# A kernel that counts its PE instructions and keeps loads of data out of a stretch of each 256

## The chip, the cores and the metric

One Trainium2 chip, one core. The metric is the device time of one execution in microseconds (us). The kernel before took 297.31 us, the median of three timed runs (295.42, 297.31 and 297.91).

The engines are named as the profile names them: PE (matmuls; PEld are its weight loads, from the same queue), DVE, ACT, POOL, and SP, which issues all DMA transfers here.

## The reference

Eight sequences of 3584 tokens, 192 channels, in two stages, all in float32. First each token's window of 7 tokens is summed with weights that are a softmax over the 7 taps, for 8 heads of 24 channels. Then a soft mixture of 8 experts with 4 slots each works on all 28672 tokens at once:

```python
# stage 1
w = softmax(weight_gen, axis=-1)                       # (B, S, 8 heads, 7 taps)
out = np.einsum('bshk,bskhg->bshg', w, x_unf)          # windows of 7 tokens
# stage 2, x is the output of stage 1 as (28672, 192)
logits = x @ phi                                       # 192 x 32
d = softmax(logits, axis=0)                            # over all tokens
slot_input = d.T @ x
slot_out[e] = np.maximum(slot_input[e] @ w1[e], 0) @ w2[e]
c = softmax(logits, axis=1)                            # over the 32 slots
return c @ slot_out
```

## The kernel before

The tokens are cut into 280 groups of 104 (35 for each sequence). One long loop runs over 70 slots of four groups (`SLOTS`). For each slot PE does the windowed sum as matmuls with banded weights (`conv`, line 264), ACT takes the result out of PSUM (`conv_out`), PE transposes it (`xpose`, line 284), ACT takes it out again. For every four slots, a unit, PE makes the logits (`logits`, line 340), DVE, PE, POOL and ACT find their running maximum and the exponentials, DVE turns these into `dt` (`dturn`, line 399), and PE sums the slot inputs (`dispatch`, line 418). In parallel the taps of later groups go through `chain`: DVE takes the maximum (`tap_top`, line 189), POOL subtracts, ACT takes the exponential, POOL and DVE sum and divide, POOL spreads them into `wide`, and DVE transposes them into the bands (`tap_turn`, line 237). After the loop come the experts (`hidden`, `outputs`) and the output stage: matmuls, eviction and stores.

Transfers of the loop, all issued by SP in one queue. `loadx` (line 162) brings the tokens: 56 slots of data in four quarters each, into four places in turn, so quarter h of slot t+4 can start when PE is through with slot t. `loadw` (line 165) brings the raw taps, 35 of them into four buffers. `loadw1` (line 485) and `loadw2` (line 488) bring the experts' weights, the latter into the places of tokens that are done with.

The order around the change is made by a planner. `op` records each piece of work with its engine and a cost in us, `model` and `times` lay them out in time, and the result `at[i]` is the planned start of piece i. The kernel is then written out in the order of `at` (lines 823 to 838). Each engine runs its own queue in that order. For PE's pieces `steps` notes the planned time at which each PE instruction ends. A load planned for later than `PACED`, 24 us, is tied by `paced` (line 818) to the PE instruction that the plan has just finished at that time: SP waits for that instruction's semaphore before it issues the load. The last eight loads of `loadw2` are left for after the loop (`later`).

A matmul in float32 shows as two weight loads and two matmuls in the trace (2,240 calls of line 264 as 4,480 of each), a transpose as one of each.

Of the kernel before, what the change touches and what calls it, by code (L numbers as in the profile page):

```python
# [33 lines left out]
PACED = 24.0  # L34
# [3 lines left out]
WGAP = 0.68  # L38
TR = 3 * 32 + T
RESTAT = 4  # L40
BEHIND = 8
ROUNDS = {"TE": 8, "SP": 12}
VSUM = ()
# [13 lines left out]
def conv_soft_moe(ctx, tc, xh, wh, phi, w1a, w1b, w2, out):  # L57
# [188 lines left out]
    def unit(p):  # L246
        return next((u, p - p0) for u, (p0, n) in enumerate(UNITS) if p < p0 + n)
# [250 lines left out]
    ops, writer, readers = [], {}, {}  # L498

    def op(eng, cost, reads, writes, f, *a, late=0.0, due=None):  # L500


        i = len(ops)
        preds = {writer[r] for r in (*reads, *writes) if r in writer}
        for r in writes:
            preds |= set(readers.get(r, ()))
            writer[r], readers[r] = i, []
        for r in reads:
            readers.setdefault(r, []).append(i)
        preds.discard(i)  # L510
        ops.append((eng, cost, late + 0.1 * (eng == "TE"), preds, due, f, a))
# [27 lines left out]
    VE, AC, PO, TE, SP = "VE", "AC", "PO", "TE", "SP"  # L539
# [141 lines left out]
    for k in range(SLOTS):  # L681
        u, i = unit(2 * k)[0], unit(2 * k)[1] // 2
# [17 lines left out]
    k = SLOTS - 2  # L700
# [104 lines left out]
    def times(start, bound):  # L805
        at, t = [0.0] * len(ops), 0.0
        for i, o in enumerate(ops):
            at[i] = t
            t += o[1] * (o[0] == bound)
        best = None  # L810
        for _ in range(ROUNDS[bound]):
            at = model(at, start, bound)
            end = max(at[i] for i, o in enumerate(ops) if o[0] == bound)
            if best is None or end < best[0]:
                best = end, at
        return best[1]

    def paced(j, by):
        if j.engine == mybir.EngineType.SP:
            tc.add_manual_dep(j, by.name, mybir.DependencyInfo(  # L820
                mybir.DependencyClass.Sync, mybir.DependencyReason.DATA), reason="paced")

    at = times({TE: 0.0, VE: 3.2, AC: 4.8, PO: 5.0, SP: 0.7}, TE)
    block = nc.cur_bb.bb
    steps, later = [], [(E - 1 - i // 4, 3 - i % 4) for i in range(BEHIND)][::-1]
    for i in sorted(range(len(ops)), key=lambda i: (at[i], i)):
        if ops[i][5] is loadw2 and ops[i][6] in later:
            continue
        n = len(block.instructions)
        ops[i][5](*ops[i][6])  # L830
        new = block.instructions[n:]
        if ops[i][0] == TE:
            new = [j for j in new if j.engine == mybir.EngineType.PE]
            steps += [(at[i] + ops[i][1] * (k + 1) / len(new), j) for k, j in enumerate(new)]
        elif ops[i][0] == SP and at[i] > PACED:
            to = max((t, k) for k, (t, _) in enumerate(steps) if t <= at[i])[1]
            for j in new:
                paced(j, steps[to][1])

    actx.close()  # L840

# [136 lines left out]
    spots += [big[:, NXS * XB - OW :]]  # L978
    assert RESTAT + 2 < len(spots)
    spots += [big[:, i * OW : (i + 1) * OW] for i in range(E * WE // OW)]  # L980
# [46 lines left out]
    def turn_two():  # L1027
        twos[0] += 1
        return ("two", twos[0] % 4)

    for j, (kind, b, g, n) in enumerate(parts):
        two, to = [turn_two(), turn_two()], ("spot", j % len(spots))
        op(TE, (1.1 + 0.8 * kind) * (n + 6) / 24, [("cT", 2 * (b + half) + (g >= STEPS[1][0])) for half in range(1 + kind)]
           + ["sob"] * kind, two, rows, kind, b, g, n, j)
        cuts = ((0, 2, AC), (2, 4, VE)) if j < 3 else ((0, 2, AC), (3, 4, VE), (2, 3, AC))
        free = ["w2"] * (j >= RESTAT + 2)
        for lo, hi, e in cuts:
# [6 lines left out]
        for lo, hi in ((0, 2), (2, 4)) if j < 3 else ((0, 4),):  # L1044
            op(SP, 0.576 * (hi - lo) * n / 18, [], [(to, c[0]) for c in cuts if lo <= c[0] < hi],
               store, j, n, lo, hi, late=2.0)
        if j == RESTAT:
            rest = turn_two()
            op(TE, 1.05, [], [rest], others, 0)
        elif j == RESTAT + 1:  # L1050
            op(TE, 1.05, [], [rest, "w2"], others, 1)
# [3 lines left out]
    at = times({TE: 0.0, VE: 0.65, AC: 0.0, PO: 0.0, SP: 0.0}, SP)  # L1055
# [93 lines left out]
```

## Time and profile before

| | us |
|---|---|
| median of three timed runs | 297.31 |
| the profiled execution's own time | 298.47 |
| its span, first to last instruction | 296.5 |
| PE matmuls busy | 259.1 |
| PE weight loads busy | 212.8 |
| DVE busy | 213.3 |
| ACT busy | 180.3 |
| POOL busy | 160.2 |

The profiled execution is 0.4% above the median of the timed ones; its span leaves out 2.0 us around the first and the last instruction. The loop over slots ends near 214 us by the chain of work that ended last; then come the experts and, from about 235 us, the output stage. The matmuls' ends are modelled, so a busy PE is not PE at its peak. "issue" as the end of a wait means that the profile shows nothing the engine waited for. The queue of DMA packets named "instruction" with the number 8 brings 16 KB packets, 55 in all.

### The profile page before, as it was taken

What the parts mean: (1) busy time and instruction counts of PE and PEld (TensorE: products, weight loads), DVE (VectorE), ACT (ScalarE), POOL (GpSimd) and SP (SyncE); (2) the same over time, 40 slices, a digit from 0 to 9 for tenths busy, and PEclk for the clock granted to TensorE, in tenths of its full rate; (3) what the DMA queues carried; (4) which work ended last, traced back from release to release, by engine and by line L of the source; (5) the groups of instructions that cost most, each with busy time, mean ns of one, the idle gap of its engine ahead of it and who ended that gap; (6) DMA issues with size and microseconds to landing.
All of it is one profiled execution on the core that took longest, in us unless ns stands there. A gap on an engine that the chain in (4) does not pass through costs nothing.

```text
span 296.5 us, 16191 instructions
## 1 busy us (share of the span) xinstructions
PE 259.1 (87%) x7032; PEld 212.8 (72%) x7032; DVE 213.3 (72%) x385; ACT 180.3 (61%) x307; POOL 160.2 (54%) x253
## 2 busy tenths in 40 slices
PE   8899899999999999998999899989989897956510
PEld 8789699888988988897998788979859652312100
DVE  8878799989978977768767778673268598977310
ACT  8887458757766764675666565655322378967430
POOL 9976669659659685475374636620016415455100
PEclk9999999999999999999999999999999999966775
DMA  6877676776767786667767757666898199999994
GB/s 188 215 217 206 204 202 205 206 217 194 213 193 203 213 226 166 189 190 206 204 178 214 218 161 201 187 180 169 259 295 266 45 345 416 412 420 416 415 418 185
DMA packets 31558, 70.11 MB, mean 236 GB/s; under 512 B 5888, under 2 KB 21248, under 8 KB 31488
## 3 DMA queue, kind: packets, MB, share of 16 engines
q1 hardware_dynamic: 31488, 69.08, 73.5%
q8 instruction: 55, 0.90, 1.4%
q14 instruction: 15, 0.12, 0.1%
HBM read 46.70 MB, written 22.36 MB: 233 GB/s over the span
## 4 chain that ended last, share of the span: by engine, by line
PE 76%; issue 5%; DMA 4%; POOL 4%; DVE 3%; ACT 3%; POOLq 0%; ACTq 0%; DVEq 0%
PE ring L264 32%; PE ring L284 16%; PE ls L340 8%; PE acb L418 8%; PE two L991 7%; DMA out<-big 3%; PE ring L901 2%; ACT big L997 2%; PE ring L923 1%; POOL big L434 1%; DMA taps<-wh 1%; POOL LT L106 1%; DVE band L237 1%; DVE cT L476 1%; PE ring L418 0%
## 5 line engine op out<-in xcount | busy, mean ns | idle before, releaser
L264 PE MATMUL ring<-big,band 128*26 128x96 f32 x4480 | 111.3, 248 | 6.4 <-issue 4.9
L264 PEld LDWEIGHTS ring<-big,band 128*26 128x26 f32 x4480 | 100.6, 130 | 14.9 <-issue 9.5
L272 ACT COPY tm<-ring 128x768 f32<-128x768 f32 x68 | 54.4, 800 | 63.4 <-PE ring L264 47.3
L237 DVE STREAM_TRANSPOSE band<-wide 128x832 f32<-128x832 f32 x70 | 70.6, 1026 | 4.4 <-POOL wide L228 3.2
L284 PE MATMUL ring<-ident,tm 122*128 122x122 f32 x408 | 50.8, 273 | 0.4 <-issue 0.4
L228 POOL TENSOR_TENSOR wide<-taps,sum 128x364 f32<-128x364 f32 x32 | 31.4, 981 | 27.5 <-DVE sum L219 10.8
L290 ACT COPY cm<-ring 128x624 f32<-128x624 f32 x68 | 44.1, 690 | 1.7 <-PE ring L284 1.6
L284 PEld LDWEIGHTS ring<-ident,tm 122*128 122x128 f32 x408 | 42.3, 141 | 3.6 <-issue 0.8
L197 POOL TENSOR_TENSOR taps<-taps,top 128x364 f32<-128x364 f32 x34 | 33.2, 980 | 6.9 <-DVE top L189 6.6
L213 POOL TENSOR_TENSOR si<-taps 128x208 f32<-128x208 f32 x34 | 21.8, 641 | 20.5 <-ACT taps L205 20.1
L991 PE MATMUL two<-cT,so 32*128 32x442 f32 (+2 forms) x136 | 21.9, 652 | 12.2 <-DVE cT L476 6.9
L189 DVE TENSOR_REDUCE top<-taps 128x52 f32<-128x364 f32 x34 | 28.0, 825 | 4.2 <-DMA taps<-wh 4.2
L418 PE MATMUL acb<-tm,dt 128*32 128x193 f32 x544 | 26.9, 328 | 1.5 <-DVE dt L399 0.9
L340 PE MATMUL ls<-cm,phi_sb 128*32 128x208 f32 x544 | 27.4, 338 | 0.0
L106 POOL TENSOR_TENSOR LT<-LT,sm 128x576 f32<-128x576 f32 (+1 forms) x16 | 18.1, 1134 | 16.0 <-DVE sm L104 16.0
L94 POOL TENSOR_TENSOR LT<-LT,rm 128x576 f32<-128x576 f32 (+1 forms) x16 | 18.1, 1131 | 15.6 <-DVE rm L92 15.4
L991 PEld LDWEIGHTS two<-cT,so 32*128 32x128 f32 x136 | 8.4, 205 | 22.9 <-ACT big L997 6.2
L219 DVE RECIPROCAL sum<-sum 128x52 f32<-128x52 f32 (+1 forms) x36 | 16.2, 453 | 10.3 <-POOL sum L215 10.1
L205 ACT ACTIVATE taps<-taps 128x364 f32<-128x364 f32 (+1 forms) x36 | 17.9, 501 | 8.2 <-POOL taps L197 8.2
L418 PEld LDWEIGHTS acb<-tm,dt 128*32 128x32 f32 x544 | 17.7, 110 | 5.4 <-issue 1.3
L340 PEld LDWEIGHTS ls<-cm,phi_sb 128*32 128x32 f32 x544 | 16.9, 109 | 5.0 <-issue 0.3
L997 ACT COPY big<-two 128x884 f32<-128x884 f32 (+3 forms) x26 | 17.1, 739 | 3.9 <-issue 3.0
(135 smaller groups left out, 294.3 us busy)
## 6 DMA issues: line engine op xcount, KB each, us to landing
big<-xh SPq DMA_DIRECT2D x224, 120.0 KB, 3.5
taps<-wh SPq DMA_DIRECT2D x35, 182.0 KB, 3.8
out<-big SPq DMA_DIRECT2D x7, 884.0 KB, 10.2
big<-w SPq DMA_DIRECT2D x32, 192.0 KB, 4.1
out<-big SPq DMA_DIRECT2D x6, 936.0 KB, 10.5
w1a_sb<-w1a SPq DMA_DIRECT2D x32, 128.0 KB, 3.5
out<-w1a_sb SPq DMA_DIRECT2D x3, 936.0 KB, 12.1
w1b_sb<-w1b SPq DMA_DIRECT2D x16, 128.0 KB, 3.5
```

Of the source, the lines that this page charges most:

```text
L189: V.tensor_reduce(out=row(m), in_=run(c, 0, KT).rearrange("p k s -> p s k"), axis=AX.X, op=ALU.max)
L197: eng.tensor_tensor(out=t, in0=t, in1=rows7(tops.pop((c, 0))), op=ALU.subtract)
L228: eng.tensor_tensor(out=dst, in0=raw[c % NTAP][:, 0:KT], in1=m.unsqueeze(1).to_broadcast([128, KT, n, T]), op=ALU.mult)
L237: V.transpose(bands[c % NBAND][:, b].rearrange("p b j l -> p (b j l)"), wide[:, b].rearrange("p b j -> p (b j)"))
L264: P.matmul(cv[32 * blk : 32 * blk + T, p % 2, o : o + 4 * GW], bands[g // 8 % NBAND][:, g // 4 % CH, :, i], xbd[:, place(t), :, b * GW : ( ...
L272: copy(tms[tm_at(u)][:, pr + of.start : pr + of.stop, 1 : 2 * D + 1], cv[:, of, 0 : 2 * D])
L284: P.transpose(pt[:, j // 3, o : o + TR], tm[0:TR, pr + j // 3, 1 + o : 129 + o], ident[0:TR, 0:TR])
L290: copy(cm.rearrange("p (a i) (b j) -> p a (i b) j", i=3, j=T), pts["t", k][:, of, 0 : 3 * 128].rearrange("p a (i j) -> p a i j", j=32)[... ...
L340: P.matmul(lp[32 * blk : 32 * blk + 32, lo:hi, par, 0:T], phi_sb[:, 2 * par + i, :], cm[:, lo:hi, 1 if i else 2 * par, blk, :], start=(i = ...
L418: P.matmul(ac[32 * q : 32 * q + 32], dt[:, g, :], tm[:, g // 2, o : o + D + 1], start=(g < 4), stop=(g + 4 >= 2 * n))
L991: P.matmul(pos[j][q // 2][m * half : m * half + m, q % 2, 0 : n * T], of[32 * q : 32 * q + 32], cT[32 * q : 32 * q + 32, g0 : g0 + n, 0:T] ...
L997: copy(to.rearrange("p (q c) -> p q c", c=n * T), pos[j][lo // 2][:, lo % 2 : lo % 2 + hi - lo, 0 : n * T])
```

## The change

While the kernel is written out, each PE instruction gets a running count: four for a matmul, two for a transpose, and 0.045 for semaphore waits, from 7 at the beginning. Loads that the plan starts after 24 us are put into a list `waiting` and written out by `send` when PE's steps have come that far. A load whose step falls on the places 140 to 212 of each 256 by that count (and whose planned time is under 198 us) is tied to the first later step outside of these places. Two loads are at least 0.44 us apart in planned time. A load that another piece needs is written out at once, before that piece. The plan itself (`op`, `model`, `times`) is as before, and so is what each engine computes.

```diff
+ISSUE, OPEN, WAITS, BLOCK, CLOSED = 0.44, 198.0, 0.045, 256, (140, 212)
...
     block = nc.cur_bb.bb
     steps, later = [], [(E - 1 - i // 4, 3 - i % 4) for i in range(BEHIND)][::-1]
+    count = [7.0]
+
+    def counted():
+        for j in block.instructions[seen[0]:]:
+            if j.engine == mybir.EngineType.PE:
+                count[0] += (2 if getattr(j, "is_transpose", False) else 4) + WAITS
+        seen[0] = len(block.instructions)
+
+    seen = [0]
+    counted()
+    waiting, sent = [], [0.0]
+
+    def send(force=False):
+        while waiting:
+            i = waiting[0]
+            t = max(at[i], sent[0] + ISSUE)
+            k = max((t0, k) for k, (t0, _, _) in enumerate(steps) if t0 <= t)[1]
+            if at[i] < OPEN and CLOSED[0] <= (steps[k][2] - 1) % BLOCK < CLOSED[1]:
+                while k < len(steps) and CLOSED[0] <= (steps[k][2] - 1) % BLOCK < CLOSED[1]:
+                    k += 1
+            if not force and (k >= len(steps) - 1 or steps[-1][0] < t):
+                return
+            k = min(k, len(steps) - 1)
+            sent[0] = max(t, steps[k][0])
+            waiting.pop(0)
+            n = len(block.instructions)
+            ops[i][5](*ops[i][6])
+            for j in block.instructions[n:]:
+                paced(j, steps[k][1])
+
     for i in sorted(range(len(ops)), key=lambda i: (at[i], i)):
         if ops[i][5] is loadw2 and ops[i][6] in later:
             continue
+        if ops[i][0] == SP and at[i] > PACED:
+            waiting.append(i)
+            send()
+            continue
+        while any(j in waiting for j in ops[i][3]):
+            send(True)
         n = len(block.instructions)
+        c = count[0]
         ops[i][5](*ops[i][6])
-        new = block.instructions[n:]
         if ops[i][0] == TE:
-            new = [j for j in new if j.engine == mybir.EngineType.PE]
-            steps += [(at[i] + ops[i][1] * (k + 1) / len(new), j) for k, j in enumerate(new)]
-        elif ops[i][0] == SP and at[i] > PACED:
-            to = max((t, k) for k, (t, _) in enumerate(steps) if t <= at[i])[1]
-            for j in new:
-                paced(j, steps[to][1])
+            new = [j for j in block.instructions[n:] if j.engine == mybir.EngineType.PE]
+            counted()
+            steps += [(at[i] + ops[i][1] * (k + 1) / len(new), j, c + (count[0] - c) * (k + 1) / len(new))
+                      for k, j in enumerate(new)]
+            send()
+    send(True)
```

## Rows read from the trace of the kernel before

**Rows 1.** The page: busy us of each engine (share of the span, instructions), and the chain of work that ended last, shares of the span by engine.

```profile
PE 259.1 (87%) x7032; PEld 212.8 (72%) x7032; DVE 213.3 (72%) x385; ACT 180.3 (61%) x307; POOL 160.2 (54%) x253
...
PE 76%; issue 5%; DMA 4%; POOL 4%; DVE 3%; ACT 3%; POOLq 0%; ACTq 0%; DVEq 0%
```

**Rows 2.** The timeline of PE's weight loads in two stretches, 59 to 62 us (the row of 61.19) and 20 to 216 us (the others): start, us, engine, line, operation, tiles, form, count, and in brackets the idle time of the weight loads ahead of it and what ended it.

```profile
32.35 0.26 PEld L264 LDWEIGHTS ring<-big,band 128*26 128x26 f32 x9 [1.59 <-issue]
...
61.19 0.19 PEld L366 LDWEIGHTS acb<-mq,sel 128*32 128x32 f32 x8 [0.66 <-POOL sum L215]
...
86.62 0.60 PEld L264 LDWEIGHTS ring<-big,band 128*26 128x26 f32 x27 [0.37 <-issue]
...
90.39 1.14 PEld L284 LDWEIGHTS ring<-ident,tm 122*128 122x128 f32 x11 [0.19 <-issue]
...
106.94 0.37 PEld L264 LDWEIGHTS ring<-big,band 128*26 128x26 f32 x16 [0.35 <-issue]
...
111.91 0.12 PEld L418 LDWEIGHTS acb<-tm,dt 128*32 128x32 f32 x3 [0.58 <-issue]
...
120.17 1.03 PEld L284 LDWEIGHTS ring<-ident,tm 122*128 122x128 f32 x10 [0.63 <-issue]
...
158.81 0.64 PEld L418 LDWEIGHTS acb<-tm,dt 128*32 128x32 f32 x20 [0.76 <-issue]
...
168.19 0.19 PEld L264 LDWEIGHTS ring<-big,band 128*26 128x26 f32 x5 [1.46 <-issue]
...
185.27 0.69 PEld L264 LDWEIGHTS ring<-big,band 128*26 128x26 f32 x32 [0.79 <-issue]
...
198.34 0.19 PEld L264 LDWEIGHTS ring<-big,band 128*26 128x26 f32 x4 [1.16 <-issue]
```

**Rows 3.** Three stretches: from and to (us), length, then for each engine (PE, PEld, DVE, ACT, POOL) its busy us and the number of its instructions, PE's granted clock, the DMA engines' busy share, GB/s.

```profile
0.00:32.34 32.34, 28.51 (x723) 26.14 (x723) 25.98 (x51) 24.43 (x39) 26.96 (x57) 1.00 0.76 207
...
32.34:168.18 135.84, 132.00 (x4047) 117.58 (x4048) 109.69 (x188) 86.79 (x148) 90.07 (x142) 1.00 0.72 202
...
168.18:197.90 29.72, 28.59 (x886) 25.86 (x885) 22.65 (x38) 17.89 (x30) 14.70 (x25) 1.00 0.63 179
```

**Rows 4.** The instructions of line 264 between 24 and 200 us: the semaphore waits in PE's queue (count; min/median/max ns; first and last start).

```profile
L264 PEldq EVENT_SEMAPHORE  x97: 51/51/51, 27.4 to 198.5; - x97
```

**Rows 5.** Eight stretches of PE, each of about 256 matmuls and weight loads, in the columns of rows 3.

```profile
82.17:86.25 4.08, 4.08 (x130) 3.88 (x125) 3.43 (x8) 2.55 (x5) 3.63 (x7) 1.00 0.70 195
154.06:158.05 3.99, 3.99 (x132) 3.78 (x126) 3.46 (x8) 2.89 (x7) 2.41 (x5) 1.00 0.78 223
...
27.39:30.77 3.38, 3.38 (x131) 3.36 (x125) 3.13 (x6) 2.07 (x4) 3.14 (x7) 1.00 0.82 243
163.32:166.74 3.42, 3.42 (x134) 3.21 (x128) 2.75 (x5) 1.72 (x4) 2.90 (x5) 1.00 0.93 245
181.17:184.48 3.31, 3.31 (x129) 3.06 (x128) 3.05 (x8) 2.08 (x4) 0.85 (x3) 1.00 0.81 218
193.85:197.18 3.33, 3.33 (x136) 3.32 (x129) 2.64 (x6) 1.43 (x3) 1.00 (x1) 1.00 0.71 205
45.33:48.66 3.33, 3.33 (x128) 2.98 (x131) 2.90 (x5) 2.83 (x6) 3.16 (x4) 1.00 0.66 192
40.83:45.31 4.48, 4.48 (x138) 3.93 (x127) 4.45 (x7) 2.79 (x6) 3.44 (x5) 1.00 0.70 195
```

**Rows 6.** The instruction queue's packets that began in four narrow stretches, in this order: 29.90 to 29.93, 41.43 to 41.46, 45.54 to 45.57 and 113.23 to 113.25 us. Packets, MB, and the time that the packet took as a share of 16 engines over the stretch.

```profile
q8 instruction: 1, 0.02, 239.0%
...
q8 instruction: 1, 0.02, 268.5%
...
q8 instruction: 1, 0.02, 193.1%
...
q8 instruction: 1, 0.02, 398.4%
```

**Rows 7.** SP's timeline in four stretches, the last issues ahead of a place: 26.4 to 30, 42 to 46, 38 to 41.5 and 109 to 114 us. Start, us, line, transfer, count.

```profile
26.49 1.92 SPq L162 DMA_DIRECT2D big<-xh  x4
...
44.57 2.28 SPq L162 DMA_DIRECT2D big<-xh  x3
...
40.40 0.35 SPq L165 DMA_DIRECT2D taps<-wh  x1
...
110.99 0.40 SPq L165 DMA_DIRECT2D taps<-wh  x1
```

**Rows 8.** DMA issues between 24 and 200 us: transfer, count, KB each, median us from issue to landing.

```profile
big<-xh SPq DMA_DIRECT2D x192, 120.0 KB, 3.5
taps<-wh SPq DMA_DIRECT2D x28, 182.0 KB, 3.8
w1a_sb<-w1a SPq DMA_DIRECT2D x32, 128.0 KB, 3.5
w1b_sb<-w1b SPq DMA_DIRECT2D x10, 128.0 KB, 3.6
```

**Rows 9.** Who waited for whom over the span: us in total, times, longest us.

```profile
DVE top L189 <- DMA taps<-wh: 4.2, 6, 1.3
```

**Rows 10.** DVE's timeline, 126 to 136 us, in the columns of rows 2.

```profile
132.46 0.90 DVE L189 TENSOR_REDUCE top<-taps 128x52 f32<-128x364 f32 x1 [0.99 <-DMA taps<-wh]
```

**Rows 11.** The timeline of PE's weight loads, 126 to 136 us, in the columns of rows 2.

```profile
134.95 1.14 PEld L418 LDWEIGHTS acb<-tm,dt 128*32 128x32 f32 x32 [1.09 <-DVE dt L399]
```

## The prediction

> **What bounds the kernel now.** I read the page's busy times and its chain first: 76% of the span's chain lies on PE [rows 1], so in the long loop (to about 214 us) time is won only where PE stands still. Next the timeline of PE's weight loads, with the idle time ahead of each stretch and what ended it. Of the idle times of 0.19 us or more between 24 and 200 us, eleven have no other work that explains them [rows 2]. Ten are put down to "issue" (nothing that the profile shows), the one at 61.19 to a POOL operation. Their idle times are 1.59, 0.66, 0.37, 0.19, 0.35, 0.58, 0.63, 0.76, 1.46, 0.79 and 1.16 us: 8.5 us together.
>
> Where do they sit? Between the restart at 32.35 and the one at 168.19 PE took 4,047 matmuls and 4,048 weight loads, up to that at 198.34 another 886 and 885 [rows 3]. With the semaphore waits of its queue (97 on the convolution's line alone [rows 4]) that is 32 and 7 times 256: the stalls return at one place of each 256 instructions. In that rhythm one 16 KB packet of the instruction queue arrives: the packet that began between 29.90 and 29.93 us filled 239% of 16 engines over 0.03 us, so it took 1.15 us [rows 6], ended near 31.06, and PE went on at 32.35, 1.3 us later [rows 2]. I read this as PE's next 256 instructions arriving late. The place before was crossed at 27.39: from there to the stall PE ran 131 matmuls and 125 weight loads [rows 5]. So that fetch began 2.5 us after the crossing. In short: a fetch that begins s after a crossing lets PE over the next one at s + 1.2 + 1.35, and PE's own need for 256 instructions is 3.3 to 3.4 us where they are mostly convolution and 4.0 to 4.5 us otherwise [rows 5]. Short blocks can afford s = 0.8, long ones s of 1.5 to 1.9.
>
> **The change: what it counts.** The code's count must meet the real place. To 32.34 us there are 723 matmuls and 723 weight loads [rows 3]; with the 7 that the code starts from, and 0.045 for each of some 380 calls (estimate: four records per call), its count there is about 1,470, less 1 and modulo 256: place 189. The closed stretch 140 to 212 thus lies some 49 instructions ahead of the crossing to 23 behind it, in time about 0.6 us ahead (at 13 ns an instruction, 3.3 us by 256), over 1 us where transposes come just ahead, to 0.3 us behind. The aim is met.
>
> **What it moves.** 262 loads are issued between 24 and 200 us [rows 8]; 72 of 256 places are closed, so about 74 loads (estimate, evenly spread) move back by at most some 1.2 us, and no two follow closer than 0.44 us in plan. SP takes 1.92 us for four [rows 7], 0.48 each, so the open 184 places of a 4.2 us block hold 6.3; the demand is 262 / 176 x 4.2 = 6.25. SP is then full in the open stretches and some loads leak into the closed ones. Work on PE, DVE, ACT and POOL is unchanged in kind and order; the counting is host code and costs nothing on the chip.
>
> **What a quiet crossing gives.** No block of before is exactly such, so I bound s from the nearest rows. Upper end: 27.39, with four transfers in the 1.92 us from 26.49 [rows 7]: s = 2.5, nothing gained. Quiet crossings: 111.91, where SP's last issue began at 110.99 [rows 2, 7], had its fetch at 113.24: s = 1.3. 40.83, where the last issue before it began at 40.40 [rows 5, 7], had it near 41.44: s = 0.6 [rows 6]. Lower end: 45.33 had s = 0.2 although SP was issuing three loads from 44.57 on [rows 5 to 7]. I take 1.2, towards the later of the quiet ones, since the moved loads make the queue ahead of the closed stretch denser. PE then crosses 3.75 us after the last crossing.
>
> Four largest stalls, blocks of 3.38, 3.42, 3.33 and 3.31 us [rows 5]: 0.37, 0.33, 0.42 and 0.44 us are left, 1.56 of 5.00: saved 3.44. The four of 0.66, 0.19, 0.35 and 0.63 us: the block from 86.62 to the stall that ended at 90.39 is 3.58 long [rows 2], so 0.17 stays; for the other three I take 3.5 (estimate, between 3.38 and 3.58), 0.25 each: 0.92 of 1.83 left, saved 0.91. The three of 0.37, 0.58 and 0.76 end blocks of 4.08, 4.39 (106.94 to 111.33) and 3.99 us [rows 2, 5]: saved whole, 1.71. Short blocks that were lucky lose: that at 45.33, 3.33 us long, now stalls 0.42, and I allow for a second: minus 0.84. Sum: 3.44 + 0.91 + 1.71 - 0.84 = **5.2 us**. At s = 0.8 about 7.9 is saved, at s = 1.6 about 1.6.
>
> **What the moved loads cost.** A moved load of x is used three slots after its own is freed; 56 slots share about 214 us, 3.8 us each, so 11 us stand against four issues of 0.48 and 3.5 us to landing [rows 8]: a delay of 1.2 us is hidden by that lead, and costs its own length if the lead is used up. Moved weights for the later layers are needed only after the loop: nothing, at the other end their own delay of up to 1.2 us. The loads of taps are tight: DVE waited for them six times, 4.2 us [rows 9]. Behind such a wait stands all of DVE's queue. The one at 132.46 (0.99 us) [rows 10] held up the transpose of dt, and PE waited 1.09 us for it [rows 11]; the others did not reach PE's list. Lower end of the cost: nothing, or the loss of that one wait (a gain of 1.1); upper end: 28 loads [rows 8] times 1.1. I take one more such wait, 1.1, and 0.3 because a PE that is not held arrives earlier at dt: **1.4 us**. The nearest row supports it: one of six waits reached PE.
>
> 5.2 - 1.4 = 3.8 us. Everything after the loop hangs on its end and moves with it. The profiled execution took 298.47 us (span 296.5), 0.4% above the median of the timed runs, 297.31; the saving taken from the median gives **293.5 us**.
>
> [...]
>
> **Rivals.**
> - *All stalls go.* With s below 0.8 even short blocks cross freely, as 45.33 shows; if no taps load is late either, 8.5 us go: 288.8. Against it: both quiet crossings average 1.0, and short blocks need less.
> - *The last issues do not set s.* 45.33 had loads issued right up to it and the earliest fetch; 111.91 had none for 0.9 us and a middling one [rows 6, 7]. Then what decides is how much was queued over several us, or when PE asks; the same loads only bunch elsewhere, stalls move to other blocks, and the time stays: 297.3. In the same place belongs the case that PE's fetch is hidden and the eleven waits have another cause; the regular place speaks against that: 297.3 too.
> - *Taps late (the other side).* Place: DVE's wait for taps, then dt, then PE. Each late one that reaches PE costs 1.1 us. From five on the 5.2 us are eaten, from eight on the kernel is slower by over 1%: 8 x 1.1 - 5.2 = 3.6, 300.9 us. For it: SP at 6.25 of 6.3 has no reserve, so delays can add up. Against it: five of six waits of this kind did not reach PE.
> - *The count misses the place.* If waits are not 0.045 an instruction the closed stretch drifts; but 32 blocks came out whole, and 70 places are wide enough for an error of 20. Counted with the second rival.
>
> **Chances.** My forecast 0.50, its own range 290.8 (s = 0.8) to 297.1 (s = 1.6); all stalls gone 0.13; last issues do not matter, or the place is missed 0.22; fetch hidden 0.03; taps late 0.12. A measurement of this kernel tells about 1% (3 us) from no change: of my forecast 0.40 lies beyond that, 0.10 within. Faster by over 1%: 0.40 + 0.13 = 0.53. Within 1%: 0.10 + 0.22 + 0.03 = 0.35. Slower: 0.12. The range of 290.0 to 298.2 leaves out most of the second and the last case, about 0.2.
>
> **What would show it.** Right: in the timeline of PE's weight loads the stalls of over 1 us are gone before 200 us and what is left comes to 2.5 to 4.5 us, at the same place of 256, at the ends of blocks below 3.6 us; instruction packets begin 0.6 to 1.5 us after a crossing; SP shows pauses of 0.6 to 1.2 us around crossings. DVE's waits for taps grow by 1 to 4 us, with one or two seen by PE. Wrong: stalls as long as before at the same place with SP quiet ahead of them (second rival); PE waiting for dt or band for over 4 us (third); a pause of SP that lies elsewhere in the 256 (count). The stalls after 200 us should stay as they are, since the plan's loads from 198 us on are left free.

## The result, and the profile after

The changed kernel took 298.2 us, the median of 20 runs (294.87 to 305.71); the kernel before, on the same chip in turn with it, 296.54 us (20 runs, 293.67 to 299.89). The ratio is 1.0061 (95% interval 1.0039 to 1.0083): 0.6% slower, where 293.5 us and a gain were forecast, and at the very edge of the range (298.2).

One warning on the traces: executions of one kernel differ by 2% and more (293.67 to 299.89 us, 294.87 to 305.71 us). The profiled one of before (298.47 us) lies 2 us above the median of 296.54, and the first one of after (294.87 us) is the lowest of its 20. Whoever compares these two pages finds a gain of 3.6 us that the timed runs don't have. The ratios below leave disturbed runs out. Another profile of after (e10_after, 298.73 us) is near its median, and the reading of the loss rests on that one.

The page of the first profile of after: its span, busy us (share of the span) of each engine, and the two large DMA queues.

```profile
span 293.0 us, 16192 instructions
...
PE 259.7 (89%) x7032; PEld 213.1 (73%) x7032; DVE 212.5 (73%) x385; ACT 180.6 (62%) x307; POOL 160.4 (55%) x253
...
q1 hardware_dynamic: 31488, 69.08, 73.7%
q8 instruction: 55, 0.90, 1.3%
```

Matmuls, weight loads and the other engines' instructions are as many as before [rows 1]. The stalls of PE's weight loads in the same profile, 24 to 200 us, in the columns of rows 2; every stretch with an idle time of 0.19 us or more:

```profile
31.43 0.26 PEld L265 LDWEIGHTS ring<-big,band 128*26 128x26 f32 x9 [0.99 <-issue]
...
52.22 0.63 PEld L419 LDWEIGHTS acb<-tm,dt 128*32 128x32 f32 x17 [0.33 <-issue]
...
69.15 0.18 PEld L265 LDWEIGHTS ring<-big,band 128*26 128x26 f32 x3 [0.25 <-issue]
...
72.87 0.19 PEld L367 LDWEIGHTS acb<-mq,sel 128*32 128x32 f32 x8 [0.82 <-POOL sum L216]
...
95.19 0.92 PEld L265 LDWEIGHTS ring<-big,band 128*26 128x26 f32 x42 [0.40 <-issue]
...
107.81 0.38 PEld L265 LDWEIGHTS ring<-big,band 128*26 128x26 f32 x16 [0.52 <-issue]
...
120.22 1.04 PEld L285 LDWEIGHTS ring<-ident,tm 122*128 122x128 f32 x10 [0.35 <-issue]
...
134.55 1.14 PEld L419 LDWEIGHTS acb<-tm,dt 128*32 128x32 f32 x32 [0.62 <-DVE dt L400]
...
165.88 0.19 PEld L265 LDWEIGHTS ring<-big,band 128*26 128x26 f32 x5 [0.70 <-issue]
...
175.13 0.26 PEld L265 LDWEIGHTS ring<-big,band 128*26 128x26 f32 x9 [0.50 <-issue]
```

Two rows of 0.20 and 0.29 us, put down to POOL, are left out. The eight "issue" stalls come to 4.04 us, against 7.88 for the ten of before [rows 2]. That is inside the 2.5 to 4.5 us that the prediction named as the sign of success, but in the fastest of 20 executions. The kernel is not faster, and two things show why.

**The closed stretch is not kept.** The restart at 31.43 us stands at the end of a block. Two windows of the first profile of after, in the columns of rows 3:

```profile
31.42:90.24 58.82, 57.98 (x1770) 51.65 (x1770) 49.94 (x88) 39.25 (x69) 41.95 (x64) 1.00 0.70 199
90.24:94.80 4.56, 4.56 (x127) 4.05 (x127) 3.86 (x7) 4.27 (x7) 4.36 (x6) 1.00 0.55 163
```

From 31.42 to 90.24 us PE takes 3,540 matmuls and weight loads; with some 44 semaphore waits that is 14 blocks of 256, so a crossing lies at about 90.25 us. The closed stretch, 49 instructions ahead of it to 23 behind, lasts from about 89.4 to 91.5 us here, since the 23 instructions behind this crossing are mostly transposes and take 1.3 us. SP's timeline around it (start, us, line, transfer, count), and the instruction packets that began in 87.45 to 87.48, 91.74 to 91.77 and 96.72 to 96.75 us (columns of rows 6):

```profile
85.79 1.75 SPq L163 DMA_DIRECT2D big<-xh  x2
87.84 1.29 SPq L486 DMA_DIRECT2D w1a_sb<-w1a  x1
89.30 0.35 SPq L166 DMA_DIRECT2D taps<-wh  x1
89.73 2.53 SPq L163 DMA_DIRECT2D big<-xh  x4
92.36 1.66 SPq L486 DMA_DIRECT2D w1a_sb<-w1a  x1
94.11 1.78 SPq L163 DMA_DIRECT2D big<-xh  x4
95.98 0.37 SPq L486 DMA_DIRECT2D w1a_sb<-w1a  x1
96.52 0.35 SPq L166 DMA_DIRECT2D taps<-wh  x1
96.96 1.36 SPq L163 DMA_DIRECT2D big<-xh  x1
```

```profile
q8 instruction: 1, 0.02, 273.1%
...
q8 instruction: 1, 0.02, 397.3%
...
q8 instruction: 1, 0.02, 255.4%
```

The packets took 273.1%, 397.3% and 255.4% of 16 x 0.03 us: 1.31, 1.91 and 1.23 us. Each ends some 0.36 us before a long issue of SP does: the same load of `w1a` that takes 0.37 us at 95.98 takes 1.29 us at 87.84 and 1.66 at 92.36. So SP stands still while PE's instructions are fetched, falls behind its ties and catches up right where it should be quiet: of the four token loads from 89.73 us on three, by their records at 89.73, 90.22 and 90.68, fall into the closed stretch.

**Taps are late.** DVE's waits for taps over the span, first profile of after, then e10_after (us, times, longest); 4.2 us in [rows 9]:

```profile
DVE top L190 <- DMA taps<-wh: 11.1, 9, 2.2
```

```profile
DVE top L190 <- DMA taps<-wh: 12.7, 11, 2.7
```

In e10_after, near the median, these waits reach PE. The stalls of its weight loads, 24 to 200 us (columns of rows 2):

```profile
31.96 0.25 PEld L265 LDWEIGHTS ring<-big,band 128*26 128x26 f32 x9 [1.05 <-issue]
...
62.30 0.19 PEld L367 LDWEIGHTS acb<-mq,sel 128*32 128x32 f32 x8 [2.09 <-POOL taps L198]
...
78.75 0.67 PEld L265 LDWEIGHTS ring<-big,band 128*26 128x26 f32 x26 [0.20 <-issue]
...
86.27 0.19 PEld L367 LDWEIGHTS acb<-mq,sel 128*32 128x32 f32 x8 [1.19 <-POOL sum L216]
...
113.58 0.12 PEld L419 LDWEIGHTS acb<-tm,dt 128*32 128x32 f32 x3 [0.64 <-issue]
...
121.83 1.03 PEld L285 LDWEIGHTS ring<-ident,tm 122*128 122x128 f32 x10 [0.63 <-issue]
...
136.64 1.14 PEld L419 LDWEIGHTS acb<-tm,dt 128*32 128x32 f32 x32 [0.82 <-DVE dt L400]
...
168.08 0.19 PEld L367 LDWEIGHTS acb<-mq,sel 128*32 128x32 f32 x8 [0.77 <-POOL si L215]
...
191.39 0.19 PEld L367 LDWEIGHTS acb<-mq,sel 128*32 128x32 f32 x8 [0.85 <-POOL taps L198]
```

By the names that the profile gives, "issue" is down to 2.52 us, and five other stalls come to 5.72 us (1.75 in the profile of before [rows 2, 11]). The one at 86.27, in the middle of a block, is the plainest. DVE's timeline of the same kernel ahead of it:

```profile
83.56 0.91 DVE L190 TENSOR_REDUCE top<-taps 128x52 f32<-128x364 f32 x1 [2.30 <-DMA taps<-wh]
84.38 1.04 DVE L238 STREAM_TRANSPOSE band<-wide 128x832 f32<-128x832 f32 x1
85.34 0.56 DVE L348 TENSOR_REDUCE mx<-ls 128x1 f32<-128x416 f32 x1
85.93 0.22 DVE L350 TENSOR_SCALAR mq<-acb,mx 128x4 f32<-128x4 f32 x1
```

DVE stood 2.30 us for the taps. Behind `tap_top` in its queue stood the maximum (lines 348 and 350) that PE's `newmax` (line 367) needs, and it was ready at 86.15 us. The profile names a POOL operation for the stall at 86.27; by time the last is DVE's of 85.93.

The largest, at 62.30, has two causes. DVE's timeline, SP's, PE's matmuls, and the instruction packet that began between 58.95 and 58.98 us (columns of rows 6):

```profile
59.63 0.88 DVE L190 TENSOR_REDUCE top<-taps 128x52 f32<-128x364 f32 x1 [2.73 <-DMA taps<-wh]
...
61.97 0.22 DVE L350 TENSOR_SCALAR mq<-acb,mx 128x4 f32<-128x4 f32 x1
```

```profile
50.22 5.08 SPq L163 DMA_DIRECT2D big<-xh  x8
...
55.94 0.35 SPq L166 DMA_DIRECT2D taps<-wh  x1
```

```profile
61.64 0.24 PE L265 MATMUL ring<-big,band 128*26 128x96 f32 x1 [1.23 <-issue]
62.33 0.25 PE L367 MATMUL acb<-mq,sel 128*32 128x5 f32 x8 [0.45 <-DVE mq L350]
```

```profile
q8 instruction: 1, 0.02, 240.8%
```

The last matmul ahead of `newmax` is the first instruction of a new block of 256. It came at 61.64 us, 1.5 us behind the end of the packet (58.96 and 1.16 us, so 60.12): up to there, 1.4 of the 2.09 us, PE stood for its instructions. Only the rest, about 0.7 us, is DVE's. The taps were issued at 55.94 us, after SP had spent 5.08 us on eight token loads, 0.64 each. So the late fetches of e10_after cost PE some 3.9 us, and the waits behind DVE some 4.3.

### The profile page after: what moved, and what is told of

The parts are those of the page before. It is cut to its first block, busy times and chain, and to the rows that moved or that the text cites. A ratio compares the mean times of both kernels' runs of the same rounds, so it can differ in the third digit from the quotient of the medians.

```text
span 293.0 us, 16192 instructions
## 1 busy us (share of the span) xinstructions
PE 259.7 (89%) x7032; PEld 213.1 (73%) x7032; DVE 212.5 (73%) x385; ACT 180.6 (62%) x307; POOL 160.4 (55%) x253
## 5 line engine op out<-in xcount | busy, mean ns | idle before, releaser
L95 POOL TENSOR_TENSOR LT<-LT,rm 128x576 f32<-128x576 f32 (+1 forms) x16 | 18.1, 1132 | 16.4 <-DVE rm L93 16.3
L419 PE MATMUL acb<-tm,dt 128*32 128x193 f32 x544 | 26.3, 328 | 0.5 <-DVE dt L400 0.4
L419 PEld LDWEIGHTS acb<-tm,dt 128*32 128x32 f32 x544 | 16.9, 110 | 4.5 <-DVE dt L400 0.8
```

Of the source, the lines that this page charges most:

```text
L419: P.matmul(ac[32 * q : 32 * q + 32], dt[:, g, :], tm[:, g // 2, o : o + D + 1], start=(g < 4), stop=(g + 4 >= 2 * n))
```

## The experiments

This table was worked out from the records of each trace, 24 to 200 us; ratios are against the kernel before, timed in turn with it, with 95% intervals. "Closed" are loads that SP really issued on places 140 to 212 of the code's count, over all its loads (evenly spread it would be 28%). "Fetch" is the mean time from a crossing to the start of the next instruction packet (40 blocks). "Taps late" is the mean time of the taps' issue behind the PE instruction that the plan of before names. "Wait" is DVE's for taps (over the span); "issue" and "other" are the sums of PE's stalls of 0.19 us or more as read above, by what the profile says ended them. The stall at the `newmax` near 61 us, right behind a crossing, stands under "other", though part of it is a late fetch as above: 0.6 of 0.7 us in before, 1.1 of 1.2 in before_again, 1.4 of 2.1 in e10_after, 0.8 of 0.9 in e2, 0.8 of 1.0 in e15. All in us.

```
kernel                  time ratio                closed   fetch  taps late  wait  issue  other
before                  1                         100/261  1.36    1.33      4.2   7.9    1.8
before_again            1                         105/259  1.18    1.58      8.0   4.0    4.5
after                   1.0061 [1.0039, 1.0083]    93/265  1.20    2.22     11.1   4.0    1.9
after_again             (one run)                  90/263  1.24    2.13     10.2   3.6    3.5
e10_after               1.0106 [1.0063, 1.0150]    90/259  1.30    2.32     12.7   2.5    5.7
e1_no_closed            1.0025 [0.9971, 1.0080]    95/262  1.52    1.48      3.2   7.0    1.7
e2_half_block           1.0038 [0.9994, 1.0083]   100/260  1.24    1.94     11.4   4.2    5.4
e3_taps_free            1.0056 [1.0014, 1.0098]    96/263  1.27    1.92      6.0   5.6    1.6
e4_no_loads             0.9717 [0.9660, 0.9775]    12/52   0.56      -       0     0.5    0
e5_half_open            0.9759 [0.9714, 0.9805]    53/177  0.95    0.50      0     1.1    0
e6_half_closed          0.9738 [0.9688, 0.9788]    36/174  0.92    1.03      0     0.9    0
e7_all_late             1.0204 [1.0147, 1.0262]   103/250  1.43    2.79     14.7   5.0    8.0
e8_all_early            0.9979 [0.9946, 1.0013]    98/265  1.31    0.51      0.7   5.7    0.4
e9_closed_early         1.0016 [0.9977, 1.0054]    88/260  1.45    0.82      0.5   6.7    0.6
e11_taps_late           0.9987 [0.9950, 1.0025]   101/261  1.36    1.86      6.7   7.8    1.2
e12_rest_late           1.0024 [0.9987, 1.0060]   104/262  1.39    1.71      7.1   5.0    2.4
e13_taps_ahead          1.0048 [1.0018, 1.0078]   100/261  1.41   -1.25      0     8.5    0.9
e15_taps_later          1.0085 [1.0038, 1.0132]    89/253  1.36    2.94     16.3   6.9    6.1
e16_closed_taps_ahead   1.0050 [1.0019, 1.0081]    88/258  1.54   -0.93      0     8.5    0.6
```

Do these stalls make up the time? Over the 19 profiles of the table the span is about 286 us plus 1.2 times the sum of "issue" and "other" (correlation 0.98; 0.93 in the 16 with all loads). In profiles of like span, e10_after (296.9 us) and the two of before (296.5), the two sums together are alike, 8.2 against 9.6 and 8.5 us: less behind fetches, more behind DVE.

Two theories run through the experiments. In the first, the closed places and the spacing make loads late, the taps above all, and this costs the time (A, L and T in the expectations). In the second, the place of the issues hardly matters, and what counts is how much is loaded or the shifted issue of the tokens (B, N and X). C and D are about fetches with half of the tokens.

### The same kernels again

No edit: each kernel once more with a profile.

> The changed kernel unaltered, for a second profile of it. In the first, PE's fetch stalls before 200 us came to some 5.8 us against 10.2 in the kernel before, DVE waited 11.1 us for taps against 4.2, and SP still issued 93 of 265 loads on the closed places. Theory A (the closed stretch does shorten PE's fetch stalls, and late taps give the gain back through DVE): this profile shows the same, with DVE's waits for taps over 8 us and at least two PE waits of over 0.5 us behind DVE. Theory B (the closed stretch is not kept, because SP is held up, so it does nothing but delay): stalls of PE between 6 and 11 us, so that the first profile was a lucky one.

> The kernel before unaltered, for a second profile. If the first one is typical, PE's fetch stalls before 200 us come to 8 to 10 us again, the mean start of a fetch lies 1.3 to 1.5 us behind PE's crossing, DVE's waits for taps are 3 to 5 us, and 30 to 40 issues of SP last over 0.7 us, each ending about 0.36 us behind a fetch.

295.35 us (median of before beside it 296.7) and 298.49 us (296.49). Each kernel has its own picture of waits and its own spread: two profiles of before have 7.9 and 4.0 us of "issue". A difference of 3 us between two single traces proves nothing here; what follows goes by ratios and by what repeats.

### e1_no_closed and e2_half_block: without the places, and with others

```diff
-ISSUE, OPEN, WAITS, BLOCK, CLOSED = 0.44, 198.0, 0.045, 256, (140, 212)
+ISSUE, OPEN, WAITS, BLOCK, CLOSED = 0.44, 198.0, 0.045, 256, (0, 0)       # e1
+ISSUE, OPEN, WAITS, BLOCK, CLOSED = 0.44, 198.0, 0.045, 256, (12, 84)     # e2
```

> The list of waiting loads and the spacing of 0.44 us stay, the closed stretch is empty. Theory A: the time of the kernel before within 0.5% (ratio 0.995 to 1.005), DVE's waits for taps near 4 us, PE's fetch stalls near 10 us. Theory B: the spacing and the moved writing-out cost what the change costs, ratio 1.003 to 1.01.

> A closed stretch of the same length, half a block away (places 12 to 84), so that loads are moved just as often and as far but not away from PE's crossing. Theory A: late taps without the saving in stalls, slower than the change by 1% or more: ratio to before 1.015 to 1.03, stalls of PE near 10 us or more. Theory B: where the stretch lies makes no difference, ratio 1.003 to 1.01 as the change.

With the spacing of 0.44 us alone the taps are issued about as in before (1.48 us behind) and the time is 1.0025, not to be told from before. With the closed stretch half a block away the taps are late again (1.94), other stalls come to 5.4 us (4.6 without the fetch's share), "issue" falls to 4.2 as in after, and the time is 1.0038. So what a closed stretch does to waits does not need the crossing; the intervals are too wide to rank the two kernels by time.

### e3_taps_free: the change without the taps

```diff
+        if ops[i][0] == SP and at[i] > PACED and ops[i][5] is loadw:
+            k = max((t0, k) for k, (t0, _, _) in enumerate(steps) if t0 <= at[i])[1]
...
+                paced(j, steps[k][1])
+            continue
```

> The change, but loads of taps are tied to the step of their planned time as before and pass the waiting list. Theory A: DVE's waits for taps fall back to about 4 us and the saving in stalls stays, ratio to before 0.985 to 0.995. Theory B: no better than the change, ratio 1.0 to 1.01, PE's fetch stalls 6 to 11 us.

The time is 1.0056 of before: no better than the change. But the taps, tied at their planned step, were still issued 1.92 us behind it, since they stand in SP's one queue behind the token loads. Freeing a tie does not free the issue; this run tells little about the taps.

### e4_no_loads, e5_half_open, e6_half_closed: what the fetch depends on

```diff
+        if (ops[i][5] is loadx and ops[i][6][0] >= 8) or (ops[i][5] is loadw and ops[i][6][0] >= 6):
+            continue                                      # e4, on before
+        if ops[i][5] is loadx and ops[i][6][0] >= 8 and ops[i][6][1] < 2:
+            continue                                      # e5 on before, e6 on after
```

> The kernel before without its loads of tokens from slot 8 on and of taps from the sixth on (the loop works on what lies in the buffers; 42 loads of weights stay of 262). It shows what the loads cost PE through its fetches at most. If fetches are late because loads stand ahead of them: fetches begin under 0.6 us behind the crossing, no stalls over 0.3 us, and the time is 8 to 12 us shorter (ratio 0.96 to 0.975). If fetches are late for a reason of their own: starts near 1.2 us as at quiet crossings, stalls of 0.3 to 0.5 us left in short blocks, ratio 0.98 to 0.99. If the stalls of the profile do not exist in timed runs: ratio 0.99 to 1.0.

> The kernel before without half of the loads of tokens (two of four quarters from slot 8 on), so that SP issues some 166 loads in place of 262 between 24 and 200 us, all other loads and the plan unaltered: what e6 is compared with. Theory C (SP has too little time left, since it stands still during each fetch): lag of issues behind their steps falls below 0.3 us in the median; fetch stalls 3 to 7 us; ratio 0.975 to 0.99. Theory D (where loads lie relative to the crossing does not matter): the same.

> The change with the same half of the loads of tokens left out. Theory C: now SP has room, under 25 issues lie on closed places, fetches begin 0.3 us or more earlier than in e5, PE's stalls are under 2 us, and the kernel is faster than e5 by 0.5 to 1.5%. Theory D: fetches begin as in e5, stalls within 1 us of it, time within 0.4% of e5.

e4 leaves out the tokens from slot 8 on and the taps from the sixth load on; e5 and e6 leave out two of four quarters of these tokens. The stretch from 24 to 200 us, e4, e5 and e6, in the columns of rows 3:

```profile
24.00:200.00 176.00, 175.75 (x5541) 159.10 (x5533) 142.35 (x248) 115.13 (x195) 113.03 (x183) 1.00 0.16 45
```

```profile
24.00:200.00 176.00, 175.53 (x5517) 158.52 (x5510) 142.43 (x248) 115.16 (x195) 113.10 (x183) 1.00 0.50 142
```

```profile
24.00:200.00 176.00, 175.39 (x5519) 158.66 (x5513) 142.39 (x248) 115.01 (x195) 113.05 (x183) 1.00 0.50 140
```

Without the loads PE idles 0.25 us of 176, and the kernel is 2.8% faster: that, some 8 us, is all that the loads left out here cost by any way. The fetch starts 0.56 us behind the crossing without them, 0.95 and 0.92 with half of the tokens, 1.2 to 1.5 with all. What the packet itself takes hardly changes (1.08 us on average in e4, 1.21 in before). With half the tokens the closed stretch is kept better (36 of 174 issues in it against 53 of 177), and the fetch starts no earlier and the time is the same. One flaw: PE's queue holds fewer semaphore waits here (119 in the trace against 167), so the code's count runs ahead, and the crossing slides from its place 192 at 28 us to 234 at 191 us. Measured from the real crossing, 49 instructions ahead to 23 behind, it is still 27 of 174 issues against 44 of 177.

The kernels with all loads settle it without this flaw. In their 16 profiles 653 crossings can be paired with a fetch. By the number of loads issued from 49 instructions ahead of the crossing to 23 behind, the fetch began on average so many us behind the crossing:

```
loads issued there    0      1      2      3      4 to 6
crossings             17     130    252    166    88
start of the fetch    1.14   1.37   1.37   1.34   1.26
```

The correlation is -0.03; single crossings scatter by 0.5 us about these means. At crossings with no issue at all it began 0.2 us earlier, and the 17 of them are too few to be sure of that. **With more load the fetch began later here (0.56, 0.9 and 1.2 to 1.5 us); where the loads were issued makes no difference that these runs show.**

### e7_all_late, e8_all_early, e9_closed_early, e10_after: the lateness without the places

e7 is before with each load (24 to 198 us) tied 1.2 us later in the plan and no closed places; e8 is before with ties 1.2 us earlier; e9 is the change from a plan 1.2 us earlier; e10 is the change itself, beside them.

```diff
+            t = max(at[i] + 1.2 * (at[i] < OPEN), sent[0] + ISSUE)          # e7, in send, ISSUE 0, CLOSED (0, 0)
-            to = max((t, k) for k, (t, _) in enumerate(steps) if t <= at[i])[1]
+            to = max((t, k) for k, (t, _) in enumerate(steps) if t <= at[i] - 1.2)[1]     # e8
-            t = max(at[i], sent[0] + ISSUE)
+            t = max(at[i] - 1.2, sent[0] + ISSUE)                            # e9
```

> No closed stretch and no spacing; every load that the plan starts between 24 and 198 us is tied 1.2 us of planned time later. Theory L (the change is slower because its loads are later): slower than the change, ratio to before 1.01 to 1.025, and in the profile DVE's waits for taps of 12 us or more. Theory N (lateness of this size is hidden): ratio 0.997 to 1.005.

> The kernel before with every load tied 1.2 us of planned time earlier. Theory L: no slower than before, ratio 0.985 to 1.0, DVE's waits for taps under 3 us. Theory N: ratio 0.997 to 1.005. If the plan's late starts keep transfers out of each other's way: 1.005 to 1.015.

> The change with every load's planned time 1.2 us earlier ahead of the closed places, so that a moved load comes about when the kernel before had it. Theory L: the loss goes, ratio 0.99 to 1.002, DVE's waits for taps back to some 4 us. Theory N, or a loss that the closed places make by themselves: as the change, 1.003 to 1.01.

> The change unaltered beside the three, for its ratio on this chip and a third profile: 1.004 to 1.008, fetches begin 1.1 to 1.3 us behind the crossing on average, DVE's waits for taps near 10 us.

Lateness alone, with no place closed, costs 2.0%, with 8.0 us of other stalls. With the plan 1.2 us earlier the changed kernel loses its tap waits (0.5 us) and its loss (1.0016). And it is not faster than e8, which has the same shift and no closed places (0.9979): the places bring no gain that can be seen even where no tap is late.

### e11 to e14: taps and tokens apart

The edit of e7 with the taps alone late (e11) or all but the taps late (e12); before with the taps up to 2.4 us ahead of their planned time in the order of SP's queue (e13), and that with all ties 1.2 us earlier (e14).

```diff
+        if ops[i][0] == SP and at[i] > PACED and ops[i][5] is not loadw:     # e11; "is loadw" in e12
...
+                paced(j, steps[k][1])                                        # tied as planned
+            continue
...
+    early = {i: max([at[i] - 2.4] + [at[p] + 1e-6 for p in ops[i][3]])       # e13, e14
+             for i in range(len(ops)) if ops[i][5] is loadw and at[i] > PACED + 2.4}
+    for i in sorted(range(len(ops)), key=lambda i: (early.get(i, at[i]), i)):
...
+            to = max((t, k) for k, (t, _) in enumerate(steps) if t <= early.get(i, at[i]))[1]          # e13
+            to = max((t, k) for k, (t, _) in enumerate(steps) if t <= early.get(i, at[i]) - 1.2)[1]    # e14
```

> The kernel before, with the loads of taps alone tied 1.2 us of planned time later and so placed behind later loads in SP's queue; no closed places. Theory T (late taps pay, through DVE): most of the 2.0% of all loads late, ratio 1.01 to 1.025, DVE's waits for taps over 12 us. Theory X (late tokens and weights pay): ratio 0.997 to 1.005.

> The kernel before, with all loads but those of taps tied 1.2 us later, which lets the taps pass them. Theory T: ratio 0.99 to 1.004, DVE's waits for taps under 5 us. Theory X: 1.01 to 1.02, with PE or POOL waiting for tokens, or fetch stalls of over 10 us.

> The kernel before, with the loads of taps up to 2.4 us of planned time earlier, in the queue's order too, as far as their buffers are free by the plan. Theory T: DVE's waits for taps under 1.5 us, no wait of PE behind DVE over 0.5 us, ratio 0.988 to 0.998. Theory X: 0.997 to 1.004.

> As e13, and every load of the paced part tied another 1.2 us earlier. Theory T: as e13, within 0.3% of it, since nothing waits for the other loads. If earlier loads stand ahead of PE's fetches more often: slower than e13 by 0.3% or more, fetch stalls over 9 us.

e11, 0.9987, speaks against the taps at first sight. In its trace their issue came only 0.5 us later than in before (1.86 against 1.33): SP had been behind anyway. It was a weak test, and e15 repeats it. e12, 1.0024: tokens that are issued 2.4 us behind the plan (2.4 in e7 too; 0.9 in before, 1.8 in after) cost little by themselves. e13 ends all waits for taps and is slower, 1.0048, with 8.5 us of "issue" stalls: moving taps up is no remedy. e14 stays inconclusive: its median, 297.18, is above that of before beside it (296.45) while its ratio, 0.9913 [0.9868, 0.9958], rests on the four lowest of its 12 runs, and the execution that was profiled took 624.86 us and is not read.

### e15_taps_later and e16_closed_taps_ahead: taps alone, and all but them

```diff
-            t = max(at[i] + 1.2 * (at[i] < OPEN), sent[0] + ISSUE)
+            t = max(at[i] + 2.4 * (at[i] < OPEN), sent[0] + ISSUE)           # e15, on e11
+        if i in early:                                                       # e16, on after, early as in e13
+            k = max((t0, k) for k, (t0, _, _) in enumerate(steps) if t0 <= early[i])[1]
...
+            continue
```

> The kernel before with nothing but the 28 loads of taps tied 2.4 us later in the plan (1.2 us moved their issue by only some 0.4 us, since SP was free by then). If late taps are what costs the changed kernel its time: taps issued on average over 2 us behind the plan, DVE waiting over 12 us for them, and the time 1.008 to 1.02 of before. If the lateness of the tokens or the denser issue costs it: 0.997 to 1.004, as with 1.2 us.

> The change as it is, closed places and all, but the loads of taps go up to 2.4 us ahead of their planned time and pass the list; tokens and weights stay as late as the change makes them. If late taps are what costs the changed kernel its time: DVE waits under 2 us for taps, and the loss is gone, 0.994 to 1.003 of before. If late tokens, or the shifted issue as such, cost it: still 1.004 to 1.011, with DVE's waits gone all the same.

e15 takes 1.0085 of before, DVE waiting 16.3 us. The larger of PE's stalls in it that are not "issue" (columns of rows 2):

```profile
62.92 0.19 PEld L367 LDWEIGHTS acb<-mq,sel 128*32 128x32 f32 x8 [1.03 <-POOL sum L216]
...
74.89 0.19 PEld L367 LDWEIGHTS acb<-mq,sel 128*32 128x32 f32 x8 [0.78 <-POOL sum L216]
...
87.18 0.19 PEld L367 LDWEIGHTS acb<-mq,sel 128*32 128x32 f32 x8 [1.09 <-POOL sum L216]
...
100.00 0.19 PEld L367 LDWEIGHTS acb<-mq,sel 128*32 128x32 f32 x8 [1.62 <-POOL si L214]
...
197.82 0.19 PEld L367 LDWEIGHTS acb<-mq,sel 128*32 128x32 f32 x8 [1.54 <-POOL taps L198]
```

All five are `newmax`, 6.1 us; of the one at 62.92, right behind a crossing, 0.8 us are a late fetch, the other four lie in the middle of a block. Late taps by themselves make such stalls and cost such a time: that is shown. e16 took the late taps out of the change: no wait for taps, 0.6 us of other stalls, and still 1.0050, which is the rival's number. Two of its stalls (columns of rows 2):

```profile
31.92 0.25 PEld L265 LDWEIGHTS ring<-big,band 128*26 128x26 f32 x9 [1.51 <-issue]
...
54.32 0.63 PEld L419 LDWEIGHTS acb<-tm,dt 128*32 128x32 f32 x17 [1.34 <-issue]
```

Its "issue" is at 8.5 us as in e13, and its time is that of e13 (1.0048): with the taps ahead, the closed places change nothing that can be seen, for better or worse.

## Why the prediction was wrong

- **Stalls at one place of 256, from a late fetch: right.** They all but vanish with the loads (0.5 us in e4, against 7.9 and 4.0 us in the two profiles of before), and 149 "issue" stalls at crossings, in the 16 profiles with all loads, end 1.2 to 1.7 us behind the end of a fetch.
- **The count meets the place: right.** No load planned before 198 us is tied to a place from 140 to 211 by the code's count, and the crossing at 90.25 us lies where the code takes it to be.
- **"The open 184 places of a 4.2 us block hold 6.3" loads, "some loads leak": wrong by size.** Of SP's issues in the first profile of after 36 took over 0.7 us, against 0.37 usually, one for most of the 42 fetches; together they held SP 33.7 us longer, 0.8 a block. Of 4.2 us 1.2 are closed and 0.8 lost: 2.2 are left, some 4.6 loads at 0.48 us (an estimate), for a demand of 6.25. The gate therefore leaks: 93 of 265 issues on closed places, 100 of 261 in before. The issue of 1.92 us for four loads [rows 7], from which I took 0.48, held no fetch.
- **"A quiet crossing gives s = 1.2", 5.2 us saved: the step that failed first.** The sum lets every block have one s, 1.2 us, and takes it for a gain. But before has that mean already: the fetch started 1.36 and 1.18 us behind the crossing in two profiles of before, and 1.20 to 1.30 in three of after. What stalls PE is the spread about the mean (from 0.4 us ahead of the crossing to 2.1 behind it in the first profile of after, 0.1 to 2.5 behind it in that of before), and the issues near the crossing don't set it: the 653 crossings above, and e6 against e5. The rival that the last issues do not set s was right; two quiet crossings and one lucky one were too few rows to choose against it. In after's profiles the "issue" stalls are few (4.0, 3.6 and 2.5 us, the last 3.9 with its share of the stall at 62.30), which looks like a saving; but e3, e9 and e16 have the closed places too, and 5.6, 6.7 and 8.5 us. The pairs that differ by the closed places without late taps show no saving: 1.0016 against 0.9979 (e9, e8), 1.0050 against 1.0048 (e16, e13), where 5.2 us would be 0.017.
- **"One more such wait", 1.4 us, for late taps: wrong by size.** The chain was right (DVE's wait, then what stands behind it in its queue, then PE), but it ran mostly into the maximum that `newmax` waits for, not into `dt`. Near the median (e10_after) it is five stalls and some 4.3 us without the fetch's share, against 1.2 us in before's first profile; before's second has 3.4 us too, so the size is not certain from traces. What repeats is the lateness: the taps are issued 2.1 to 2.3 us behind the plan in three profiles of after, 1.3 and 1.6 in before, and DVE waits 10 to 13 us against 4 and 8. e15, at 2.9 us, costs 0.85% by late taps alone; e9, at 0.8 us, has lost the loss.
- **Moved tokens are hidden: about right.** e12: 1.0024 with tokens 2.4 us late.
- **The sum at s = 0.8** comes to some 8.4 us when it is redone by the prediction's own blocks, not 7.9; nothing above hangs on it.

So the gain did not come and the price of the third rival was paid in part: between the 297.3 of the one and the 300.9 of the other.

What stays open: how the 0.6% divides. e15, e7 and e9 put it on late taps; e16 does not recover it, but neither would the taps ahead be free in before (e13), and why they cost 0.5% there, with 8.5 us of "issue" stalls, was not settled. That fewer fetch stalls go with late taps, since a PE that waits for DVE gives the next fetch time, is a guess of mine: it would fit much of the table (not e15), but no run tests it.

## What to carry to other kernels

This gate on when transfers are issued did not hold, since the issuing queue had no slack at that very moment: 93 of 265 issues fell on closed places, and with half of the tokens 36 of 174 (e6). Ahead of such a gate, work out the queue's open time with the longest issues in the trace, not the usual ones, and look afterwards where the issues really fell. Before delaying loads, list those whose consumer stands at the head of a queue that the bound engine also needs; here taps that were issued 1.0 us later on average (2.32 against 1.33 us behind the plan, e10_after and before) went with a PE stall of 1.19 us at 86.27 us, where the fetch at 31.96 us made one of 1.05. When single executions differ by as much as the effect, take several profiles, choose one near the median, and let pairs of kernels that differ in one thing decide.

## What the runs showed of the hardware that was not expected

- SP's DMA issue stood still while PE's instruction packet was transferred: 37 issues of over 0.7 us for 41 fetches in before, 36 for 42 in after; from the 10th to the 90th percentile such an issue ended 0.36 to 0.37 us after a packet's end in after. Beyond the usual 0.37 us an issue this held SP 35.7 us of 176 in before, 33.7 in after.
- The fetch began later, the more was loaded: 0.56 us behind the crossing without the loads of e4, 0.9 with half of the tokens, 1.2 to 1.5 with all, while its own length stayed at 1.1 to 1.2 us. With all loads it began on average 1.3 us behind the crossing when four to six loads were issued and not landed, 1.6 us when seven or eight were.
- PE went on 1.2 to 1.7 us, 1.4 in the median, behind the end of the packet that it waited for (149 stalls).
